# Placing the transposes of h and of a later tile of x between the products of the experts' second layer

## The chip, the cores and the metric

One core of a Trainium2 chip runs the whole program in one launch. The metric is device time in microseconds (us) of that core, as the median of several executions. The kernel before takes 1447.33 us (three runs, 1446.78 to 1450.29). One more execution was profiled; it took 1446.02 us, of which the span from the first to the last instruction is 1444.1 us. All durations below come from that execution.

The engines are named as in the profile: PE (TensorE, matrix products), PEld (the loading of PE's weights, which overlaps PE), DVE (VectorE), ACT (ScalarE), POOL (GpSimd) and SP (SyncE, which issues most DMAs).

## The reference

```python
x = attention(q, k, v)                 # 4608 tokens, 512 features
# experts: one of 8 per token
logits = x @ w_gate
e_idx  = argmax(logits)
for e in range(8):
    h  = maximum(x[mask] @ w1[e], 0)   # 512 -> 1024
    ye = h @ w2[e]                     # 1024 -> 512
    out[mask] = gate_w * eom * ye
# a dense layer pair after it
g = s * maximum(x @ w_in, 0)**2 + b    # 512 -> 2048
y = g @ w_out                          # 2048 -> 512
```

All tensors are float32. The change touches the experts only.

## The kernel before

The program has three stages on PE: attention with the router (to about 200 us of the span), the experts (200 to 680 us) and the dense pair (680 us to the end). Instructions of each engine run in the order in which the code issues them; a hand-written order decides what stands where, and no planner moves it.

The experts work on tiles of 128 tokens, sorted by expert and padded; there are 39 such tiles for these inputs. `gather(i)` (POOL, an indirect DMA) fetches tile i into one of two buffers `xg`. `tr(i)` turns it on PE: four transposes of 128x128 into the PSUM tile `pt`, which `split` (ACT, then DVE) cuts into a high and a low part `xh`, `xl` in float32r. `l1(i)` is the first layer: 24 products of 512 columns, 12 into `bank[0]` and 12 into `bank[1]`; behind the first 12 ACT makes `hs[0]` with a relu (L1032), behind the second DVE makes `hs[1]` (L1034). `trh()` turns both halves of h: eight transposes into the PSUM tiles `th0`, `th1`; `cut_h` splits these into `hh` and `hl`, which are the weights of the 24 products of the second layer, `l2` (L1058, into `py`).

The layers are skewed by one tile. One round of the loop, `slot(i)`, is on PE: the 24 products of `l1(i)`; the 24 products of `l2` for tile i-1; eight transposes of h of tile i; four transposes of x of tile i+2. From the 36th tile on the number of tiles is known only at run time: `close` and `more` write one branch (`tc.If(total > i)`) inside the other, and there the transposes of h stand first behind the branch. Behind the last of these branches `finish_h`, in the tail, turns and splits the last h, and the last second layer follows at once.

Beside PE, a round on ACT and DVE is in this order: the relus; the split of a later x; if the expert changes, four pieces of the split of new w1 (`sw1`); the copy of `py` of the round before; a step of preparing the dense weights (`side`, `db.step`, with POOL); the split of h; if the expert changes, four pieces of the split of new w2 (`sw2`); another step of `side`. So everything that `sw2` and `side` put there stands ahead of the next round's relus on ACT and DVE.

Of the kernel before, what the change touches and what calls it, by code (L numbers as in the profile page):

```python
# [9 lines left out]
F32 = mybir.dt.float32  # L10
# [17 lines left out]
DM = H * D  # L28
# [3 lines left out]
P = 128  # L32
# [476 lines left out]
NSLOT = NT + E - 1  # L509
# [293 lines left out]
def split(nc, hi, lo, raw, eng=None):  # L803
    nc.scalar.activation(out=hi, in_=raw, func=AF.Copy)  # L804
    (eng or nc.vector).tensor_tensor(out=lo, in0=raw, in1=hi.bitcast(F32), op=ALU.subtract)
# [173 lines left out]
def experts(ctx, tc, c, kp, wt, xd, ys, bank, wide, side, ahead, tail):  # L979
    nc = tc.nc  # L980
    ident = c["ident"]
    p1 = ctx.enter_context(tc.tile_pool(name="ex1", bufs=1))
    p2 = ctx.enter_context(tc.tile_pool(name="ex2", bufs=2))
    ps = ctx.enter_context(tc.tile_pool(name="exps", bufs=2, space=PSUM))
    ps1 = ctx.enter_context(tc.tile_pool(name="exps1", bufs=1, space=PSUM))


    def room(name, dt, n=2):
        return [p1.tile([P, DM], I32, name=f"{name}{i}").bitcast(dt) for i in range(n)]

    xg = room("xg", F32)
    xs = list(zip(room("xh", F32R), room("xl", F32R)))
    hs = room("hs", F32)
    hh, hl = room("hh", F32R), room("hl", F32R)

    def words(t):

        return t.bitcast(U16).rearrange("p (d w) -> p w d", w=2)

    def planes(t):  # L1000

        return t.bitcast(U16).rearrange("p (w d) -> p w d", w=2)

    def apart(dst, src, engines):
        for w, copy in enumerate(engines):
            copy(out=planes(dst)[:, w], in_=words(src)[:, w])

    def gather(i):
        nc.gpsimd.indirect_dma_start(
            out=xg[i % 2], out_offset=None, in_=xd[:, :],  # L1010
            in_offset=bass.IndirectOffsetOnAxis(ap=kp["idx"][:, i:i + 1], axis=0),
        )

    def tr(i):
        a = xg[i % 2]
        pt = ps.tile([P, DM], F32, tag="pt", name="pt")
        for k in range(4):
            nc.tensor.transpose(out=pt[:, k * P:k * P + P], in_=a[:, k * P:k * P + P], identity=ident)
        return lambda: split(nc, *xs[i % 2], pt)

    def l1(i):
        xh, xl = [x.rearrange("p (k n) -> p k n", n=P) for x in xs[i % 2]]
        wh, wl = [w.rearrange("p (k f) -> p k f", f=FE) for w in wt.a]
        for n in range(2):
            s = slice(n * 512, n * 512 + 512)
            ph = bank[n]
            for k in range(4):
                nc.tensor.matmul(ph, lhsT=xh[:, k], rhs=wh[:, k, s], start=k == 0, stop=False)  # L1028
                nc.tensor.matmul(ph, lhsT=xh[:, k], rhs=wl[:, k, s], start=False, stop=False)  # L1029
                nc.tensor.matmul(ph, lhsT=xl[:, k], rhs=wh[:, k, s], start=False, stop=k == 3)  # L1030
            if n == 0:
                nc.scalar.activation(out=hs[n], in_=ph, func=AF.Relu)  # L1032
            else:
                nc.vector.tensor_scalar(out=hs[n], in0=ph, scalar1=0.0, scalar2=None, op0=ALU.max)  # L1034

    def trh():

        th = []
        for n in range(2):
            pt = ps1.tile([P, DM], F32, tag=f"th{n}", name="th")  # L1040
            for k in range(4):
                nc.tensor.transpose(out=pt[:, k * P:k * P + P], in_=hs[n][:, k * P:k * P + P], identity=ident)  # L1042
            th.append(pt)
        return th

    def cut_h(th):
        for n in range(2):
            split(nc, hh[n], hl[n], th[n])

    def l2(py, end=False):  # L1050
        wh, wl = [w.rearrange("p (k f) -> p k f", f=DM) for w in wt.b]
        ah, al = [[h[k // 4][:, k % 4 * P:k % 4 * P + P] for k in range(8)] for h in (hh, hl)]
        steps = [[(ah[k], wh[:, k]), (ah[k], wl[:, k]), (al[k], wh[:, k])] for k in range(8)]
        if end:
            steps = [[s[0] for s in steps], [s[1] for s in steps], [s[2] for s in steps]]
        steps = [s for part in steps for s in part]
        for j, (a, w) in enumerate(steps):
            nc.tensor.matmul(py, lhsT=a, rhs=w, start=j == 0, stop=j == len(steps) - 1)  # L1058
        return py

    def room_y():
        return ps.tile([P, DM], F32, tag="py", name="py")

    def result(i, py, end=False):

        y = wide() if end else p2.tile([P, DM], F32, tag="y", name="y")
        apart(y, py, [nc.scalar.copy, nc.vector.tensor_copy])
        r = nc.values_load(kp["st"][0:1, i:i + 1], engines=[ENG.SP], min_val=0, max_val=N - 1)
        nc.sync.dma_start(out=ys[bass.ds(r, P), :], in_=y.bitcast(U16))

    def sw1(i):
        wt.switch(0, kp["chg"][0:1, i:i + 1], kp["nxt"][0:1, (i and i + 1):(i and i + 1) + 1], i == 0)

    def sw2(i):
        wt.switch(1, kp["chg"][0:1, i:i + 1], kp["nxt"][0:1, (i and i + 1):(i and i + 1) + 1], i == 0)

    def second(i):

        e = nc.values_load(kp["nxt"][0:1, 1:2], engines=[ENG.SP], min_val=0, max_val=E - 1)
        for j in range(4):  # L1080
            wt.load(i, bass.ds(e, 1), part=j)

    gather(0)
    gather(1)
    tr(0)()
    gather(2)
    sw1(0)
    tr(1)()
    gather(3)
    wt.split(1)  # L1090
    sw2(0)
    total = None


    later = []

    def first(i):
        l1(i)
        if i < 2:
            second(i)  # L1100
        if later:
            later.pop(0)()
        if i + 1 < NSLOT:
            sw1(i + 1)
        while later:
            later.pop(0)()

    def slot(i):
        first(i)
        if i >= 1:  # L1110
            py = l2(room_y())
        th = trh()
        if i + 2 < NSLOT:
            later.append(tr(i + 2))
        side(i, 0)
        gather(i + 4)
        cut_h(th)
        if i >= 1:
            sw2(i)
            later.append(lambda: result(i - 1, py))  # L1120
        side(i, 1)

    for i in range(NT - 1):
        if i == NT - 2:
            total = nc.values_load(
                kp["total"][0:1, 0:1], engines=[ENG.PE, ENG.Activation, ENG.DVE, ENG.SP, ENG.Pool],
                min_val=NT, max_val=NSLOT,
            )
        slot(i)


    py = room_y()

    def close(i):
        first(i)
        if i < NT:
            tr(i + 2)()
            gather(i + 4)
        l2(py)
        sw2(i)  # L1140

    def more(i):

        if i == NSLOT:
            return
        with tc.If(total > i):
            cut_h(trh())
            if NT < i < NSLOT - 1:
                tr(i + 1)()
                if i + 3 < NSLOT:  # L1150
                    gather(i + 3)
            result(i - 2, py)
            close(i)
            more(i + 1)

    i = NT - 1
    close(i)
    side(i, 0)
    side(i, 1)
    ahead(NT, 0)  # L1160
    more(NT)

    def finish_h():
        cut_h(trh())

    def before():
        result(NSLOT + 1, py, True)

    def second_layer():
        end = room_y()  # L1170
        l2(end, True)
        return lambda: result(NSLOT, end, True)

    tail(finish_h, before, second_layer, hs, xg, lambda: p2.tile([P, DM], F32, tag="y", name="y"))


# [55 lines left out]
class Dense:  # L1232
# [93 lines left out]
    def cut(self, j):  # L1326
        hi, lo = self.cut_steps(j)
        self.later([hi], [lo])
# [139 lines left out]
    def side(self, n, j):  # L1468


        q, p = divmod(n, NPAIR)
        if q == 0 and 1 <= p < 5 and j % 2 == 0:
            self.db.step()
        if q + 1 == NGRP:
            return
        if (n, j) == (1, 0):
            n = GT * P
            self.features(self.next, [self.next[:, 4 * n:5 * n], self.extra[:, 0:n], self.extra[:, n:2 * n]])
        plan = PLAN0 if q == 0 else PLAN
        for what, k in plan.get((p, j), []):  # L1480
            getattr(self, what)(*((q + 1, k) if what in ("load", "join") else () if k is None else (k,)))
        if p == NPAIR - 1:
            self.cut(j)
# [165 lines left out]
```

## Time and profile before

| what | value |
|---|---|
| median of three runs | 1447.33 us |
| profiled execution / its span | 1446.02 / 1444.1 us |
| PE busy, share of the span | 1412.4 us, 98% |
| DVE, ACT, POOL busy | 828.1, 709.4, 429.3 us |
| products of the second layer (L1058) | 936, median 389 ns each by their records |
| transposes of h (L1042) | 312, median 272 ns by their records |
| transposes of x (L1018) | 160, median 273 ns by their records |

The record of a PE instruction is longer than its turn, since one begins while the one before still drains. What PE can issue is read from the distance of starts, not from the records' lengths. A timeline row that merges several instructions gives the first start and the stretch to the last end.

### The profile page before, as it was taken

To read this page: it belongs to the slowest core of one execution; us is meant where nothing else is said; L and a number is where in the kernel's file an instruction comes from. 1 tells how busy PE (TensorE), PEld (TensorE's weight loads), DVE (VectorE), ACT (ScalarE), POOL (GpSimd) and SP (SyncE) were. 2 spreads that over 40 slices of the span, in tenths; PEclk is the share of its full clock that TensorE was granted. 3 is DMA by queue.
4 is the path that set the end of the run, shared out by engine and by line. 5 is a ranking of instruction groups with operands and counts; after the bars stand their busy time and mean duration, and the time that the engine had idled before them with its cause. 6 is when DMAs were issued, how large, how long until landed. Compare 5 with 4: busy or idle time off the path is not lost.

```text
span 1444.1 us, 23042 instructions
## 1 busy us (share of the span) xinstructions
PE 1412.4 (98%) x7612; PEld 1243.0 (86%) x7612; DVE 828.1 (57%) x1669; ACT 709.4 (49%) x1318; POOL 429.3 (30%) x579
## 2 busy tenths in 40 slices
PE   6999999999999999999999999999999999999998
PEld 5898978888888888887888988888888888889887
DVE  6788885487746567324666534634554463455333
ACT  3666623365534355223556555545555554555443
POOL 4998233444655558325320100000010000001001
PEclk9999999999999999999999999999999999999999
DMA  9995343277865768485665654465465446545441
GB/s 248 282 316 172 125 168 127 88 234 225 234 199 184 215 192 254 144 64 153 220 163 131 181 145 127 121 189 139 117 182 147 121 129 182 138 117 162 121 115 62
DMA packets 203040, 239.43 MB, mean 166 GB/s; under 512 B 66702, under 2 KB 114062, under 8 KB 202894
## 3 DMA queue, kind: packets, MB, share of 16 engines
q1 hardware_dynamic: 195502, 217.22, 54.2%
q0 software_dynamic: 7392, 20.49, 4.7%
q8 instruction: 63, 1.03, 0.3%
q14 instruction: 83, 0.68, 0.2%
HBM read 184.39 MB, written 43.83 MB: 158 GB/s over the span
## 4 chain that ended last, share of the span: by engine, by line
PE 44%; issue 8%; DVE 0%; ACT 0%; POOL 0%; DMA 0%; POOLq 0%; DVEq 0%; ACTq 0%
PE po L1439 8%; PE po L1438 8%; PE po L1437 7%; PE bank L1378 7%; PE bank L1379 7%; PE bank L1380 7%; PE py L1058 0%; POOL out L1449 0%; DMA ring<-ws 0%; DVE yo L1446 0%; POOLq L1645 0%; DVE y L1393 0%; ACT wb L1402 0%; DVE wb L1404 0%; ACT xg L1384 0%
## 5 line engine op out<-in xcount | busy, mean ns | idle before, releaser
L1401 ACT ACTIVATE r<-r,s_b 128x384 f32<-128x384 f32 x188 | 133.3, 709 | 275.4 <-DVE r L1394 247.8
L1449 POOL DMA_INDIRECT out<-yo,kp_pos x36 | 35.7, 991 | 662.9 <-ACT yo L1448 537.2
L1439 PE MATMUL po<-wo,wb 128*128 128x512 f32 x576 | 228.6, 397 | 0.0
L1438 PE MATMUL po<-wo,wb 128*128 128x512 f32 x576 | 227.6, 395 | 0.0
L1437 PE MATMUL po<-wo,wb 128*128 128x512 f32 x576 | 224.0, 389 | 0.0
L1058 PE MATMUL py<-wb,hh 128*128 128x512 f32 x624 | 191.2, 389 | 0.3 <-ACT hh L804 0.3
L1393 DVE TENSOR_TENSOR r<-bank,held 128x384 f32<-128x384 f32 x141 | 78.4, 556 | 183.1 <-PE bank L1380 181.1
L1378 PE MATMUL bank<-wa,ring 128*128 128x384 f32 x480 | 162.3, 338 | 1.0 <-ACT xg L1384 0.9
L1379 PE MATMUL bank<-wa,ring 128*128 128x384 f32 x480 | 162.1, 338 | 0.0
L1380 PE MATMUL bank<-wa,ring 128*128 128x384 f32 x480 | 161.0, 335 | 0.0
L1404 DVE TENSOR_TENSOR wb<-r,wb 128x384 fp32r<-128x384 f32 x188 | 105.3, 560 | 67.8 <-ACT wb L1402 67.4
L1058 PEld LDWEIGHTS py<-wb,hh 128*128 128x128 f32 x624 | 117.0, 188 | 24.7 <-ACT hh L804 0.5
L804 ACT ACTIVATE hh<-th 128x512 fp32r<-128x512 f32 x78 | 42.5, 595 | 180.1 <-PE th L1042 179.0
L1439 PEld LDWEIGHTS po<-wo,wb 128*128 128x128 f32 x576 | 107.9, 187 | 23.1
L1028 PE MATMUL bank<-wa,xh 128*128 128x512 f32 x312 | 125.5, 402 | 0.0
L931 POOL TENSOR_SCALAR dt<-dt 128x256 f32<-128x256 f32 x64 | 71.9, 1123 | 175.3 <-DVE dt L930 148.9
L1030 PE MATMUL bank<-wa,xl 128*128 128x512 f32 x312 | 122.1, 391 | 0.0
L1029 PE MATMUL bank<-wa,xh 128*128 128x512 f32 x312 | 121.6, 390 | 0.2 <-DVEq L856 0.2
L1058 PE MATMUL py<-wb,hl 128*128 128x512 f32 x312 | 120.5, 390 | 0.0
L1437 PEld LDWEIGHTS po<-wo,wb 128*128 128x128 f32 x576 | 108.2, 188 | 11.5
L1438 PEld LDWEIGHTS po<-wo,wb 128*128 128x128 f32 x576 | 107.9, 187 | 11.5
L1378 PEld LDWEIGHTS bank<-wa,ring 128*128 128x128 f32 x480 | 90.1, 188 | 16.2 <-ACT r L1390 4.6
(262 smaller groups left out, 2846.5 us busy)
## 6 DMA issues: line engine op xcount, KB each, us to landing
ring<-ws SPq DMA_DIRECT2D x336, 256.0 KB
wr<-in_moe_w SPq DMA_DIRECT2D x72, 512.0 KB
ws<-wf SPq DMA_DIRECT2D x16, 896.0 KB
ys<-y SPq DMA_DIRECT2D x37, 256.0 KB
xd<-x SPq DMA_DIRECT2D x36, 256.0 KB
q<-in_q SPq DMA_DIRECT2D x16, 512.0 KB
vr<-in_v SPq DMA_DIRECT2D x8, 1024.0 KB
dx<-in_moe_w_out SPq DMA_DIRECT2D x32, 256.0 KB
```

The costliest lines, as they stand in the source:

```text
L1028: nc.tensor.matmul(ph, lhsT=xh[:, k], rhs=wh[:, k, s], start=k == 0, stop=False)
L1029: nc.tensor.matmul(ph, lhsT=xh[:, k], rhs=wl[:, k, s], start=False, stop=False)
L1030: nc.tensor.matmul(ph, lhsT=xl[:, k], rhs=wh[:, k, s], start=False, stop=k == 3)
L1058: nc.tensor.matmul(py, lhsT=a, rhs=w, start=j == 0, stop=j == len(steps) - 1)
L1378: nc.tensor.matmul(o, lhsT=w[:, 0, k], rhs=xh[:, k], start=f, stop=False, skip_group_check=True)
L1379: nc.tensor.matmul(o, lhsT=w[:, 0, k], rhs=xl[:, k], start=False, stop=False, skip_group_check=True)
L1380: nc.tensor.matmul(o, lhsT=w[:, 1, k], rhs=xh[:, k], start=False, stop=False, skip_group_check=True)
L1401: lambda: nc.scalar.activation(out=r, in_=r, func=AF.Identity, scale=s_b[:, 0:1], bias=s_b[:, 1:2]),
L1404: [lambda: nc.vector.tensor_tensor(out=gl, in0=r, in1=gh.bitcast(F32), op=ALU.subtract)],
L1437: nc.tensor.matmul(o, lhsT=gh[:, s], rhs=wh, start=first, stop=False)
L1438: nc.tensor.matmul(o, lhsT=gh[:, s], rhs=wl, start=False, stop=False)
L1439: nc.tensor.matmul(o, lhsT=gl[:, s], rhs=wh, start=False, stop=last)
```

## The change

The four transposes of a tile become a list of steps (`turns`), which `l2` takes as `among`. `l2` issues one of them behind the 4th product, the 5th, the 7th, the 8th and so on: two of three products are followed by a transpose, until the list is used up. In a round of `slot` the list holds the eight of h and the four of x, and its last one stands behind the 20th product. In `close` it holds the eight of h alone, so they now stand ahead of the branch; those of x stay in a row (`tr_now`). In the first round, which has no second layer, they stay in a row. `th0` and `th1` are allocated once. `cut_h` stays where it was.

```diff
+    def turns(pt, a):
+        return [
+            lambda k=k: nc.tensor.transpose(out=pt[:, k * P:k * P + P], in_=a[:, k * P:k * P + P], identity=ident)
+            for k in range(4)
+        ]
     def tr(i):
-        a = xg[i % 2]
         pt = ps.tile([P, DM], F32, tag="pt", name="pt")
-        for k in range(4):
-            nc.tensor.transpose(out=pt[:, k * P:k * P + P], in_=a[:, k * P:k * P + P], identity=ident)
-        return lambda: split(nc, *xs[i % 2], pt)
+        return turns(pt, xg[i % 2]), lambda: split(nc, *xs[i % 2], pt)
...
+    th = [ps1.tile([P, DM], F32, tag=f"th{n}", name="th") for n in range(2)]
     def trh():
...
+        return [f for pt, h in zip(th, hs) for f in turns(pt, h)]
...
         for j, (a, w) in enumerate(steps):
             nc.tensor.matmul(py, lhsT=a, rhs=w, start=j == 0, stop=j == len(steps) - 1)
+            if among and j >= 2 and (j % 3 != 2 or len(among) >= len(steps) - j - 1):
+                among.pop(0)()
...
     def slot(i):
         first(i)
+        among = trh()
+        if i + 2 < NSLOT:
+            steps, cut = tr(i + 2)
+            among += steps
+            later.append(cut)
         if i >= 1:
-            py = l2(room_y())
-        th = trh()
-        if i + 2 < NSLOT:
-            later.append(tr(i + 2))
+            py = l2(room_y(), among)
+        else:
+            for f in among:
+                f()
         side(i, 0)
         gather(i + 4)
-        cut_h(th)
+        cut_h()
...
     def close(i):
         first(i)
         if i < NT:
-            tr(i + 2)()
+            tr_now(i + 2)
             gather(i + 4)
-        l2(py)
+        l2(py, trh())
         sw2(i)
     def more(i):
...
         with tc.If(total > i):
-            cut_h(trh())
+            cut_h()
...
     def finish_h():
-        cut_h(trh())
+        cut_h()
```

On PE, in a round of the loop, the end of the second layer before (`py` is the second layer's output, `th` and `pt` the turned h and x, `bank` the first layer's output):

```order
L1058 MATMUL py<-wb_2839,hh_2887 128x512
L1058 MATMUL py<-wb_2840,hh_2887 128x512
L1058 MATMUL py<-wb_2839,hl_2889 128x512
L1042 MATMUL th<-ident,hs_2884 128x128 x4
L1042 MATMUL th<-ident,hs_2885 128x128 x4
L1018 MATMUL pt<-ident,xg_2878 128x128 x4
L1028 MATMUL bank_2860<-wa_114,xh_2881 128x512
```

And of the changed kernel, on PE, the beginning of the second layer of a round (hs_2884 is `hs[0]`, made by ACT; hs_2885 is `hs[1]`, made by DVE):

```order
L1065 MATMUL py<-wb_2839,hh_2886 128x512
L1017 MATMUL th<-ident,hs_2884 128x128
L1065 MATMUL py<-wb_2840,hh_2886 128x512
L1017 MATMUL th<-ident,hs_2884 128x128
L1065 MATMUL py<-wb_2839,hl_2888 128x512
L1065 MATMUL py<-wb_2839,hh_2886 128x512
L1017 MATMUL th<-ident,hs_2885 128x128
L1065 MATMUL py<-wb_2840,hh_2886 128x512
```

The transposes moved from behind the 24th product to places from behind the 4th to behind the 20th: the first that reads `hs[0]` stands 20 products earlier, the first that reads `hs[1]` 14 products earlier.

On PE in the tail, behind the last branch, before:

```order
L1146 UNCONDITIONAL_BRANCH x7
L1042 MATMUL th<-ident,hs_2884 128x128 x4
L1042 MATMUL th<-ident,hs_2885 128x128 x4
L1058 MATMUL py<-wb_2839,hh_2886 128x512 x4
L1058 MATMUL py<-wb_2839,hh_2887 128x512 x4
```

And on PE at the same place in the changed kernel:

```order
L1160 UNCONDITIONAL_BRANCH x7
L1065 MATMUL py<-wb_2839,hh_2886 128x512 x4
L1065 MATMUL py<-wb_2839,hh_2887 128x512 x4
```

The eight transposes of the last h are no longer between the branch and the last second layer.

## Rows read from the trace of the kernel before

**Rows 1.** Page, part 1: busy us, share of the span, instructions.
```profile
PE 1412.4 (98%) x7612; PEld 1243.0 (86%) x7612; DVE 828.1 (57%) x1669; ACT 709.4 (49%) x1318; POOL 429.3 (30%) x579
```

**Rows 2.** Windows, 33 rounds: stretch, length, PE PEld DVE ACT POOL busy, PEclk, DMA.
```profile
220.98:625.13 404.15, 404.15 (x1984) 339.13 (x1982) 248.54 (x415) 182.06 (x309) 208.87 (x232) 1.00 0.63 184
```

**Rows 3.** Timeline of PE, one round: start us, length us, engine, line, tiles, count.
```profile
300.04 0.61 PE L1058 MATMUL py<-wb,hh 128*128 128x512 f32 x2
...
305.25 0.40 PE L1058 MATMUL py<-wb,hl 128*128 128x512 f32 x1
305.48 1.04 PE L1042 MATMUL th<-ident,hs 128*128 128x128 f32 x8
306.36 0.60 PE L1018 MATMUL pt<-ident,xg 128*128 128x128 f32 x4
306.71 0.47 PE L1028 MATMUL bank<-wa,xh 128*128 128x512 f32 x1
307.03 0.39 PE L1029 MATMUL bank<-wa,xh 128*128 128x512 f32 x1
...
309.11 0.39 PE L1029 MATMUL bank<-wa,xh 128*128 128x512 f32 x1
...
318.96 0.48 PE L1028 MATMUL bank<-wa,xh 128*128 128x512 f32 x1
```

**Rows 4.** Timeline of PEld: loads of four transposes within the row.
```profile
306.25 0.47 PEld L1018 LDWEIGHTS pt<-ident,xg 128*128 128x128 f32 x4
```

**Rows 5.** Timeline of the first round, where transposes waited for the second relu.
```profile
207.15 0.69 DVE L1034 TENSOR_SCALAR hs<-bank 128x512 f32<-128x512 f32 x1
...
207.89 0.42 PEld L1042 LDWEIGHTS th<-ident,hs 128*128 128x128 f32 x4 [0.97 <-DVEq L856]
207.89 0.66 PE L1042 MATMUL th<-ident,hs 128*128 128x128 f32 x4 [0.73 <-DVEq L856]
```

**Rows 6.** Timeline of PE: where the second layer begins in four rounds.
```profile
324.53 0.61 PE L1058 MATMUL py<-wb,hh 128*128 128x512 f32 x2
...
471.49 0.39 PE L1058 MATMUL py<-wb,hh 128*128 128x512 f32 x1
...
544.97 0.39 PE L1058 MATMUL py<-wb,hh 128*128 128x512 f32 x1
...
557.22 0.39 PE L1058 MATMUL py<-wb,hh 128*128 128x512 f32 x1
```

**Rows 7.** Timeline of ACT and DVE: the relus of these rounds (three of ACT).
```profile
325.76 0.58 ACT L1032 ACTIVATE hs<-bank 128x512 f32<-128x512 f32 x1
...
327.80 0.68 DVE L1034 TENSOR_SCALAR hs<-bank 128x512 f32<-128x512 f32 x1
...
473.95 0.68 DVE L1034 TENSOR_SCALAR hs<-bank 128x512 f32<-128x512 f32 x1
...
546.99 0.57 ACT L1032 ACTIVATE hs<-bank 128x512 f32<-128x512 f32 x1
...
549.07 0.68 DVE L1034 TENSOR_SCALAR hs<-bank 128x512 f32<-128x512 f32 x1
...
560.39 0.58 ACT L1032 ACTIVATE hs<-bank 128x512 f32<-128x512 f32 x1
...
561.53 0.68 DVE L1034 TENSOR_SCALAR hs<-bank 128x512 f32<-128x512 f32 x1
```

**Rows 8.** Timeline: what ran ahead of the late relus on ACT and POOL.
```profile
306.12 1.09 ACT L804 ACTIVATE hh<-th 128x512 fp32r<-128x512 f32 x2 [2.56 <-PE th L1042]
...
546.12 0.96 ACT L804 ACTIVATE wf<-wf 128x896 fp32r<-128x896 f32 x1 [2.09 <-POOL wf L976]
...
553.85 5.65 POOL L976 TENSOR_TENSOR wf<-wf 128x128 f32<-128x128 f32 x4
```

**Rows 9.** Timeline of PE behind the last branch: the last transposes and second layer.
```profile
673.69 1.06 PE L1042 MATMUL th<-ident,hs 128*128 128x128 f32 x8 [0.62 <-PEq L1146]
675.06 1.20 PE L1058 MATMUL py<-wb,hh 128*128 128x512 f32 x4 [0.30 <-ACT hh L804]
```

More of the change, by code (lines that the diff above doesn't have):

```diff
@@ L1012, in gather, with tr_now @@
         )
+    def turns(pt, a):
[3 more added lines that the diff above has]
+        ]
     def tr(i):
-        a = xg[i % 2]
         pt = ps.tile([P, DM], F32, tag="pt", name="pt")
-        for k in range(4):
-            nc.tensor.transpose(out=pt[:, k * P:k * P + P], in_=a[:, k * P:k * P + P], identity=ident)
-        return lambda: split(nc, *xs[i % 2], pt)
+        return turns(pt, xg[i % 2]), lambda: split(nc, *xs[i % 2], pt)
+    def tr_now(i):
+        steps, cut = tr(i)
+        for f in steps:
+            f()
+        cut()
     def l1(i):
@@ L1034, in l1, with cut_h, l2 @@
                 nc.vector.tensor_scalar(out=hs[n], in0=ph, scalar1=0.0, scalar2=None, op0=ALU.max)
+    th = [ps1.tile([P, DM], F32, tag=f"th{n}", name="th") for n in range(2)]
     def trh():
[L1038 to L1046, printed above, removed]
+        return [f for pt, h in zip(th, hs) for f in turns(pt, h)]
+    def cut_h():
         for n in range(2):
             split(nc, hh[n], hl[n], th[n])
-    def l2(py, end=False):
+    def l2(py, among=(), end=False):
+        among = list(among)
         wh, wl = [w.rearrange("p (k f) -> p k f", f=DM) for w in wt.b]
@@ L1084, in experts @@
     gather(1)
-    tr(0)()
+    tr_now(0)
     gather(2)
     sw1(0)
-    tr(1)()
+    tr_now(1)
     gather(3)
@@ L1109, in slot @@
         first(i)
+        among = trh()
[3 more added lines that the diff above has]
+            later.append(cut)
         if i >= 1:
-            py = l2(room_y())
-        th = trh()
-        if i + 2 < NSLOT:
-            later.append(tr(i + 2))
+            py = l2(room_y(), among)
+        else:
+            for f in among:
+                f()
         side(i, 0)
         gather(i + 4)
-        cut_h(th)
+        cut_h()
         if i >= 1:
@@ L1146, in more @@
         with tc.If(total > i):
-            cut_h(trh())
+            cut_h()
             if NT < i < NSLOT - 1:
-                tr(i + 1)()
+                tr_now(i + 1)
                 if i + 3 < NSLOT:
@@ L1170, in second_layer @@
         end = room_y()
-        l2(end, True)
+        l2(end, end=True)
         return lambda: result(NSLOT, end, True)
```

## The prediction

> **What bounds the kernel now.** I read the page's busy shares first: PE is busy 98% of the span [rows 1]. That alone doesn't say that every stretch hangs on PE, so I took the windows of the 33 rounds of the expert loop: PE is busy 404.15 of 404.15 us at a granted clock of 1.00 (the 2.4 GHz level), while DVE has 61%, ACT 45%, POOL 52% [rows 2]. In these rounds PE never waits. Whatever the change adds to PE's issue, or makes PE wait, therefore lengthens the run one for one, as the dense stage behind it is not waiting for anything that arrives by clock time. What waits in these rounds is ACT and DVE, for PE.
>
> Then I read one round by its starts [rows 3]. Products of 512 columns follow each other at 5.21 us / 23 = 0.2265 us (300.04 to 305.25). Eight transposes take 305.48 to 306.36, 0.110 us each; the finer value from the loads below is 0.109. A round is 12.25 us (306.71 to 318.96); 48 products and 12 transposes at these paces are 10.87 + 1.31 = 12.18. The missing 0.07 lies around the row of transposes: 0.23 instead of 0.2265 into it, and behind it nine products from 307.03 to 309.11 at 0.231 each, 0.04 over; two hundredths of that are rounding of starts.
>
> **Part 1: PE's pace.** 34 rounds of the loop move 12 transposes each, four `close` rounds move 8 each: 440 in all. None is removed. Is one cheaper when it stands alone between products? Its load already hides behind the product in front of it (the row begins 0.23 after the last product), and in the row the transposes follow at 0.109, not held by their loads: where PE had waited for the second relu, four loads took 0.42 us from first begin to last end [rows 5], against 0.47 within a row [rows 4], so the first two were 0.06 apart, while the four transposes took 0.66 [rows 5] against 0.60 in a row [rows 3]. The load needs about 0.06, the transpose itself 0.109. The product behind it needs its own load meanwhile; the product behind the last transpose of a row began really at about 306.80 (its successor at 307.03 less one pace), which is 0.11 behind that transpose. So a lone transpose still costs 0.11, and I see no gain.
>
> There is a small loss. Products near transposes run at 0.231 instead of 0.2265, and the row's entrance costs 0.005. With transposes behind two of three products, the 18 products from the 4th to the 21st are all near one: 18 x 0.0045 = 0.08, and 12 entrances and exits of about 0.005 in place of one pair, partly the same time. I take 0.10 per round (0.07 with eight): 34 x 0.10 + 4 x 0.07 = **+3.7 us**. Bounds: 0, if a lone transpose leaves the pace alone; and 0.25 per round, 8.5 us, if each leaves twice what the row shows. A whole 0.07 for each lone one (26 us) is not possible, since most of it lies on nine following products and here one or two follow. I take the value next to the measured 0.231.
>
> The products of the first layer behind it keep a disturbed stretch as before, since the last transpose stands only four products ahead of them.
>
> **Part 2: waits for the relus.** Before, the first transpose stood 24 products behind the first layer. Now the first of `hs[0]` stands behind the 4th product of the second layer and the first of `hs[1]` behind the 10th product and four transposes. With S the start of the second layer, PE gets there at S + 4 x 0.2265 = S + 0.91 and at S + 10 x 0.2265 + 4 x 0.109 = S + 2.70. From a relu's end to the transpose pass 0.05 (207.84 to 207.89), and its load of 0.06 is then in the open [rows 5]: 0.11. In most rounds both relus are long done: ACT's and DVE's wait only for the bank. But where w2 of a new expert is being split, or `side`'s pieces pile up, they come late. Four rounds matter; S from [rows 6], the relus' ends from [rows 7]:
>
> - S = 324.53: hs[0] ends 326.34, wanted 325.44: 0.90 + 0.11 = 1.01. hs[1] ends 328.48, wanted 327.23 + 1.01 = 328.24: 0.35 more. Together 1.4.
> - S = 471.49: hs[1] ends 474.63, wanted 474.19: 0.55.
> - S = 544.97: hs[0] ends 547.56, wanted 545.88: 1.79. hs[1] ends 549.75, wanted 549.46 after that wait: 0.40. Together 2.2.
> - S = 557.22: hs[0] ends 560.97, wanted 558.13: 2.95; hs[1] at 562.21 is then in time.
>
> Two corrections. First, `hh[1]` can no longer begin behind the transposes; it must wait until the last product has read the old one. Before, the pair of splits ended at 307.21 [rows 8], 0.41 behind the round's real start. Now the last product drains 0.16 into the round, plus 0.03 and one split of about 0.6: 0.8. ACT's chain behind it (the split of w2, then the relu) is 0.39 later where nothing else holds it, as at 471.49: 0.55 + 0.39 = 0.9. In the other three it is held otherwise: at 544.97 ACT waited 2.09 us for POOL's sums of the dense weights just ahead of the relu [rows 8]. Second, PE reaches the round of 557.22 some 2.2 us later because of the wait before it, while the POOL sums that end at 559.50 [rows 8] and hold ACT there don't wait for PE. That leaves 0.75 for hs[0]; DVE's own chain, which starts from `hh` and so from PE, moves along, and makes hs[1] late instead. Between 0.75 and 2.95 I take 2.0, nearer to the upper row, because DVE's splits dominate there.
>
> Sum: 1.4 + 0.9 + 2.2 + 2.0 = **+6.5 us** (bounds 4.9 and 8.5). Behind the waiting transpose on PE's queue stand the rest of the second layer and the whole next round; nothing passes it.
>
> **Part 3: what becomes earlier.** In the tail the eight transposes are gone from behind the last branch. Before, the last began at 673.69 + 1.06 - 0.27 = 674.48; the second layer could have followed at 674.59 and did at 675.06, for want of `hh` [rows 9]. ACT will have split it while PE still finishes the layer before and crosses the branch: **-0.5 us**. The 0.62 us at the branch stays. Elsewhere the branches show no gap that the transposes filled. `hh[0]` and the x tile's split are ready sooner, but nothing waits for them: the next reader is a first layer away. The transposes of x come about 1.8 us earlier and the gather for them was issued two rounds, 24.5 us, before: nothing. POOL's next gather can start sooner; nothing waits for it either. No DMA is added or moved on SP's queue.
>
> **Sum.** 3.7 + 6.5 - 0.5 = 9.7 on the profiled execution's 1446.02: 1455.7. The median of the runs is 1.31 above that execution, so I forecast 1457.0.
>
> **Rivals.**
> - *The transposes were held by their loads, and alone they hide* (faster). Each would give back the part of 0.109 that its load needs beyond its own pass. By the two stretches of loads (0.47 and 0.42) that part is 0.05: 440 x 0.05 = 22 us, 1425. For it: the same work, spread over products under which loads hide. Against it: the loads that came 0.06 apart, and the following product's load, which takes the transpose's place as the holder. It decides from a lone transpose costing under 0.09. The Trainium skill ("TensorE: Matmul & The Clock Gate", LDWEIGHTS) gives columns / 1.2, 107 ns for 128 columns, and under "Back-to-back issue gap" 56 ns for a pass of 128 columns; by these a row would be held by its loads at about the pace seen, and lone ones would save up to 51 ns each, an estimated 22 us. The trace disagrees on which of the two is the long one.
> - *The relus arrive in time*, since the waits of PE shift or DVE's earlier `hl[0]` pulls its chain forward. Only the pace is lost: 1447.33 + 3.7 - 0.5 = 1450.5. For it: DVE's first split of h can move up. Against: ACT's late relus hang on POOL and on w2.
> - *Nothing moves*: the slow products are not due to the transposes, and the waits are absorbed: 1447.
> - *Waits spread*: each of seven expert changes pays what the worst round shows, 7 x 2.95 = 20.7, plus 3.2: 1471. Against: most changes leave the relus early enough.
>
> **How the numbers follow.** The forecast (waits and pace) 0.66; in-time relus 0.14; nothing 0.08; faster by hidden loads 0.04; spread waits 0.08. What a measurement of this kernel can tell from no change is 0.3%, 4.3 us, that is up to 1451.7. The forecast's own bounds are 4.9 + 0 - 0.5 = 4.4 and 8.5 + 8.5 - 0.5 = 16.5, 1451.7 to 1463.8; the in-time case ends at 1450.5. Range 1449 to 1464, which leaves out the faster case, no change and most of the spread. Slower: the forecast less 0.01 and the spread, 0.73. Within: the in-time case and nothing, with the forecast's lowest end, 0.22. Faster: 0.05.
>
> **What would show it.** In the profile after: a lone transpose between two products adds 0.11 to 0.12 to the distance of their starts (0.06 would prove the first rival); a quiet round takes 12.30 to 12.40 instead of 12.25; PE has idle time before transposes of h put down to the two relus, of 1 to 3 us in rounds that lie near 325, 545 and 557; the last second layer starts with hardly a wait behind the branch. Wrong would be: quiet rounds shorter than 12.2, or no idle time at these rounds.

## The result, and the profile after

The changed kernel takes 1455.8 us (median of six runs, 1454.78 to 1458.01), the kernel before 1447.62 us beside it (six runs, 1446.59 to 1450.29). The ratio is 1.0055, 95% interval 1.0042 to 1.0068: 8.2 us slower. Forecast was 1457.0, in a range of 1449 to 1464.

The profiled execution has a span of 1453.9 us, 9.8 over that of before. Of these, 1.0 lie ahead of the first round of the experts (its first product starts at 201.52, before at 200.51), in code that the change doesn't touch (in the traces of the first four variants below, that start lies between 199.05 and 201.45); 8.8 lie behind that, nearly all in the rounds. From the first round's products on, the two traces can be compared stretch by stretch.

First the stretch of [rows 2] in the changed kernel: the same 33 rounds, with the same columns.

```profile
222.18:634.89 412.71, 409.16 (x1981) 326.83 (x1980) 248.95 (x415) 184.76 (x308) 204.66 (x233) 1.00 0.62 180
```

It is 412.71 us in place of 404.15: 8.6 of the 8.8. PE is no longer busy throughout, 3.55 us of idle time have come in, and the granted clock is still 1.00. So there are two losses: idle time, and 5.0 us in which PE is busy with the same instructions for longer.

The view of waits of the changed kernel, PE from the first round on, says whom the idle time is put down to (us in total, times, longest):

```profile
PE th L1017 <- ACT hs L1042: 2.3, 3, 1.5
PE th L1017 <- DVE hs L1044: 1.1, 3, 0.5
PE py L1065 <- ACT hh L804: 1.0, 1, 1.0
PE th L1017 <- DVEq L856: 0.7, 1, 0.7
```

The first two are the relus, in the places that the prediction named; the third is the tail; the last is the first round, which waits for its second relu before as well ([rows 5]). To size a wait, idle time is not enough: the product ahead of it drains about 0.16 us into the idle stretch, and the load of the transpose stands in the open behind it. The rounds' lengths show both. A quiet round takes 12.353 us (median of 33 rounds in the trace, by the start of its first product); the five rounds that are longer take 0.89 (near 326), 0.15 (near 364), 0.73 (near 476), 2.01 (near 550) and 1.35 us more (near 565), 5.1 in all. So of the 8.6 us in [rows 2]'s stretch 5.1 are waits and 3.4 are a slower pace.

The longest wait, on the timeline of PE and of ACT, the round that answers to the third of [rows 6] and [rows 7]:

```profile
550.52 0.62 PE L1065 MATMUL py<-wb,hh 128*128 128x512 f32 x2
...
551.20 0.39 PE L1065 MATMUL py<-wb,hh 128*128 128x512 f32 x1
553.06 0.33 PE L1017 MATMUL th<-ident,hs 128*128 128x128 f32 x1 [1.47 <-ACT hs L1042]
...
555.25 0.33 PE L1017 MATMUL th<-ident,hs 128*128 128x128 f32 x1
```
```profile
551.57 0.95 ACT L804 ACTIVATE wf<-wf 128x896 fp32r<-128x896 f32 x1 [1.73 <-POOL wf L976]
552.42 0.58 ACT L1042 ACTIVATE hs<-bank 128x512 f32<-128x512 f32 x1
```

The second layer begins at 550.52 and reaches the first transpose at 551.43; the relu ends at 553.00, and the transpose starts at 553.06. As before, ACT's relu stood behind a split that waited for POOL's sums. The other 20 products of the layer, and all that follows, stood behind the transpose on PE's queue.

Now the other half, a quiet round on PE's timeline (it answers to [rows 3]):

```profile
408.46 0.40 PE L1038 MATMUL bank<-wa,xh 128*128 128x512 f32 x1
...
414.60 0.40 PE L1065 MATMUL py<-wb,hh 128*128 128x512 f32 x1
414.83 0.28 PE L1017 MATMUL th<-ident,hs 128*128 128x128 f32 x1
414.86 0.48 PE L1065 MATMUL py<-wb,hh 128*128 128x512 f32 x1
415.18 0.27 PE L1017 MATMUL th<-ident,hs 128*128 128x128 f32 x1
415.20 0.48 PE L1065 MATMUL py<-wb,hl 128*128 128x512 f32 x1
415.52 0.39 PE L1065 MATMUL py<-wb,hh 128*128 128x512 f32 x1
...
420.82 0.40 PE L1038 MATMUL bank<-wa,xh 128*128 128x512 f32 x1
```

Three products and two lone transposes take 414.60 to 415.52, 0.92 us; three products at 0.2265 and two transposes at 0.109 would be 0.90. A product "starts" 0.03 behind the transpose, but that is only its record: it is 0.48 long in place of 0.39. When it really began is seen on the timeline of the loads:

```profile
414.60 0.14 PEld L1017 LDWEIGHTS th<-ident,hs 128*128 128x128 f32 x1
414.83 0.19 PEld L1065 LDWEIGHTS py<-wb,hh 128*128 128x128 f32 x1
414.97 0.14 PEld L1017 LDWEIGHTS th<-ident,hs 128*128 128x128 f32 x1
415.18 0.19 PEld L1065 LDWEIGHTS py<-wb,hl 128*128 128x128 f32 x1
415.29 0.19 PEld L1065 LDWEIGHTS py<-wb,hh 128*128 128x128 f32 x1
```

In these rows a load begins when the instruction ahead of it takes its turn, not earlier. The transpose's load hides behind the product (414.60, used at 414.83). The product's load begins with the transpose (415.18), and the next load, which marks the product's own beginning, comes 0.11 later (415.29). Where the next load is a transpose's it comes 0.14 later (414.83 to 414.97), so the mark is good to about 0.03. So the transpose costs its 0.11 alone as well as in a row.

### The profile page after: what moved, and what is told of

Its sections match the earlier page's. It is cut to its first block, busy times and chain, and to the rows that moved or that the text cites. A ratio compares the mean times of both kernels' runs of the same rounds, so it can differ in the third digit from the quotient of the medians.

```text
span 1453.9 us, 23119 instructions
## 1 busy us (share of the span) xinstructions
PE 1414.1 (97%) x7612; PEld 1225.6 (84%) x7612; DVE 829.7 (57%) x1669; ACT 712.7 (49%) x1318; POOL 424.6 (29%) x579
## 4 chain that ended last, share of the span: by engine, by line
PE 43%; issue 8%; ACT 1%; POOL 0%; SPq 0%; DMA 0%; DVE 0%; POOLq 0%; ACTq 0%; DVEq 0%
PE po L1453 8%; PE po L1452 8%; PE po L1451 7%; PE bank L1392 7%; PE bank L1393 7%; PE bank L1394 7%; POOL out L1463 0%; DMA ring<-ws 0%; SPq L1379 0%; ACT wb L1416 0%; ACT y L1415 0%; ACT r L1415 0%; POOLq L1659 0%; ACT yo L1462 0%; ACT xg L1398 0%
## 5 line engine op out<-in xcount | busy, mean ns | idle before, releaser
L1065 PE MATMUL py<-wb,hh 128*128 128x512 f32 x624 | 220.1, 424 | 1.0 <-ACT hh L804 1.0
L804 ACT ACTIVATE hh<-th 128x512 fp32r<-128x512 f32 x78 | 46.6, 599 | 191.5 <-PE py L1065 176.6
L1065 PE MATMUL py<-wb,hl 128*128 128x512 f32 x312 | 139.7, 451 | 0.0
L1039 PE MATMUL bank<-wa,xh 128*128 128x512 f32 x312 | 121.6, 390 | 0.3 <-DVEq L856 0.3
L1038 PE MATMUL bank<-wa,xh 128*128 128x512 f32 x312 | 121.9, 391 | 0.0
L805 DVE TENSOR_TENSOR hl<-th,hh 128x512 fp32r<-128x512 f32 x78 | 52.8, 686 | 94.8 <-ACT hh L804 53.9
```

## The experiments

Each of the first four ran beside the kernel before, on one chip (1447.32 us, median of 35 runs). "Quiet round" is the median length of the 33 rounds in the run's trace, and "waits" the sum of what longer rounds take above it. In the kernel before, the rounds alternate between 12.252 and 12.241: median 12.252, mean 12.247. Each variant has one profiled execution, so its waits are those of one execution.

### Same places, x first

This is the run x_first.

```diff
-            among += steps
+            among = steps + among
```

> The changed kernel with the same 12 places, but the four transposes of x take the first four places and the eight of h the last eight. The pattern of lone transposes is the same, only what they wait for is later. Theory (waits for the relus and a slower pace, each its own term): a quiet round stays at 12.35 us as in the changed kernel, and the waits shrink, since hs[0] is now wanted at S + 2.75 and hs[1] at S + 4.55: nothing in the rounds near 326 and 476, about 0.2 in the one near 550, 1.0 to 1.4 in the one behind it; 1.2 to 1.6 in all in place of 5.1. Median about 1452.5 (1447.6 + 3.7 + 1.4). Rival 1 (all of the loss is waits, the pace only looks slower): about 1449. Rival 2 (all of the loss is pace, the idle time is given back later): 1455.8 as the changed kernel.

Measured: 1450.55 us, ratio 1.0021 (1.0010 to 1.0032). Quiet round 12.353, as in the changed kernel; waits 0.19 and 0.75 in the rounds that answer to the last two of [rows 6], 0.94 in all, a little under what was expected. The view of waits of this run has one relu left:

```profile
PE py L1065 <- ACT hh L804: 0.8, 1, 0.8
PE th L1017 <- ACT hs L1042: 0.5, 1, 0.5
```

The pattern of lone transposes costs the same and the waits are nearly gone, so the two terms are separate. Neither is given back elsewhere: from the start of the stretch of [rows 2] to the end of the trace this run takes 4.4 us more than the kernel before, and its 33 rounds alone 4.5. So both rivals fall, the first by the trace alone: its 1449 lies inside the interval of the median, and the 1452.5 of the theory just outside. The median moved by 5.2 from the changed kernel's 1455.8; by waits it should have moved by 4.2, and the two were not timed side by side. One of the waits that are gone is not to the credit of the places: near 326 the relu of `hs[0]` ends only 0.10 behind the second layer's start in this run, in time for the old places too (see Waits below).

### All in a row behind the 10th product

This is the run row_early.

```diff
-            if among and j >= 2 and (j % 3 != 2 or len(among) >= len(steps) - j - 1):
+            while among and j == 9:
```

> All 12 transposes (eight in the branches) in one row behind the 10th product of the second layer. Theory: the pace is that of the kernel before (quiet round 12.25 us), but the waits are there: hs[0] wanted at S + 2.27, hs[1] at S + 2.70, which gives about 1.0 to 1.3 in the round near 326, 0.8 near 476, 2.1 near 550 and 1.4 to 2.0 in the one behind it: 5.3 to 6.3 us in all, median 1452.9 to 1453.9. Rival 1 (all pace): 1447.6. Rival 2 (a row in the middle of the second layer slows the products on both sides, also without waits): a quiet round above 12.30.

Measured: 1451.02 us, ratio 1.0023 (1.0009 to 1.0036). Quiet round 12.247; waits 0.80, 0.20, 0.81, 2.16 and 0.80 in the same five rounds, 4.8 in all, under the 5.3 to 6.3 that were expected, because the last of them came out at 0.80 in place of 1.4 to 2.0; the median is 2 to 3 us under. PE's timeline in the worst round:

```profile
550.35 0.66 PE L1017 MATMUL th<-ident,hs 128*128 128x128 f32 x4 [0.21 <-ACT hs L1042]
552.53 0.66 PE L1017 MATMUL th<-ident,hs 128*128 128x128 f32 x4 [1.53 <-DVE hs L1044]
```

The waits are there without a single lone transpose, now mostly for DVE's relu. And a row in the middle of the second layer is no dearer than one behind it: the pace depends on the row being whole, not on its place.

### Only ahead of the branches

This is the run row_last.

```diff
-            if among and j >= 2 and (j % 3 != 2 or len(among) >= len(steps) - j - 1):
+            while among and j == len(steps) - 1:
```

> The changed kernel's code with all transposes in one row behind the last product, so that only one part of the change is left: in the branches the transposes of h stand ahead of the branch, not behind it. Theory: a quiet round 12.25 us, no waits for the relus, the time of the kernel before within 1 us (1446.6 to 1448.6). Rival (the move ahead of the branches carries a part of the loss or gives something back): 1 us or more beside it, visible in the rounds from the 36th on and in the tail.

Measured: 1447.23 us, ratio 0.9997 (0.9985 to 1.0009). Quiet round 12.252, no waits; 36th to 38th round 12.295, 12.225 and 12.253, to the nanosecond those of before. Placing the transposes of h ahead of the branches carries nothing of the loss.

### Pairs

```diff
-            if among and j >= 2 and (j % 3 != 2 or len(among) >= len(steps) - j - 1):
+            for _ in range(2 if j % 3 == 1 and j >= 3 else 0):
```

> The transposes stand in pairs, behind the 5th, 8th, 11th, 14th, 17th and 20th product (six pairs, four in the branches), otherwise the changed kernel. Theory as in the prediction (each product near a transpose runs at 0.231 in place of 0.2265, whatever stands between): all products from the 5th to the 23rd are still near one, a quiet round 12.33 to 12.35. Rival (the loss is paid per change between transposes and products): six changes in place of twelve, a quiet round 12.28 to 12.30. The waits are a little smaller than in the changed kernel, since hs[0] is wanted at S + 1.13 and hs[1] at S + 2.95: 4 to 5 us. Median 1454 to 1455.5 by the theory, 1452.5 to 1453.5 by the rival.

Measured: 1451.8 us, ratio 1.0035 (1.0022 to 1.0047). Quiet round 12.307; waits 0.53, 1.86 and 0.69, 3.1 in all, under the 4 to 5 that were expected: near 326 there is none, since the relu of `hs[0]` ends 0.10 behind the second layer's start in this run too. The timeline of a quiet round, two starts of the first layer and one pair:

```profile
404.37 0.39 PE L1038 MATMUL bank<-wa,xh 128*128 128x512 f32 x1
...
410.94 0.38 PE L1017 MATMUL th<-ident,hs 128*128 128x128 f32 x2
411.08 0.48 PE L1065 MATMUL py<-wb,hl 128*128 128x512 f32 x1
411.39 0.63 PE L1065 MATMUL py<-wb,hh 128*128 128x512 f32 x2
411.86 0.38 PE L1017 MATMUL th<-ident,hs 128*128 128x128 f32 x2
...
416.67 0.39 PE L1038 MATMUL bank<-wa,xh 128*128 128x512 f32 x1
```

Over 12.247 of one row, that is 0.060 with six stretches of transposes and 0.106 with twelve: 0.012 and 0.010 for each stretch beyond the first. The round lies outside both ranges, as the median lies under both, nearer the rival's 12.28 to 12.30 than the prediction's 12.33 to 12.35. So the loss goes mostly with the number of changes between transposes and products. Products near transposes are slow in this run as well: the two from 411.39 to the pair at 411.86 take 0.235 each. The part on the pace below sets the two against each other.

### Only x, alone, and what holds a transpose

Three runs (x_lone, x_row_16 and x_lone_16), each timed once (1446.67, 1442.65 and 1451.57 us beside 1446.64); the rounds' lengths carry the verdict. In the first, the four transposes of x stand alone, and h stays in a row behind the last product.

```diff
+            if among and j >= 15 and j % 3 != 2:
+                among.pop(0)()
...
+            py = l2(room_y(), steps)
+        for f in trh():
+            f()
```

> Only the four transposes of x stand alone among the products (behind the 16th, 17th, 19th and 20th); those of h are in one row behind the last product, in the branches too. Theory (0.009 us per change between a transpose and products, as the pairs showed): four changes more than the kernel before, a quiet round 12.28 to 12.30 us, no wait for a relu. Rival (the prediction's wording: products near transposes run slow): seven products near them, 12.28 as well at the low end, but then the two runs below must lie apart from it by whole passes.

Quiet round 12.287 (12.273 and 12.287 alternate), no waits: four stretches more, 0.008 to 0.009 each. This is at the low end of what the theory expects and is the rival's 12.28 as well, so this run alone does not tell them apart.

In the second and third, the transposes of x were replaced by 2-byte ones of a constant tile, in the row and alone.

```diff
+            lambda k=k: nc.tensor.transpose(out=pb[:, k * P:k * P + P], in_=c["ones"], identity=id16)
```

> Order of the kernel before, but from the third tile on the four transposes of x are replaced by four of a constant 2-byte tile (left out: the turning of x; its layers then compute on constants). It measures what holds transposes in a row. Theory (a row is held by each transpose's own pass, 0.109 for 4 bytes, about 0.055 for 2): three of the four shorten, the fourth is still held by the 0.11 load of the product behind it: a quiet round 12.08 to 12.12 us. Rival (loads hold the row, and a load takes as long as before): 12.25.

> As the run x_lone, with the same 2-byte transposes in place of those of x, each alone among the products (left out: the turning of x). Theory (behind a lone transpose the next product waits for its own weights, whose load of 0.11 begins only when the transpose begins, so that the pass no longer matters): a lone one still costs 0.11 to 0.12, and a quiet round stays at 12.26 to 12.31, about 0.2 above the row of the same transposes. Rival (a lone transpose costs its own pass): 12.08 to 12.12.

The row, on PE's timeline, with the round's two starts:

```profile
402.97 0.48 PE L1048 MATMUL bank<-wa,xh 128*128 128x512 f32 x1
...
414.00 1.04 PE L1017 MATMUL th<-ident,hs 128*128 128x128 f32 x8
414.87 0.39 PE L1030 MATMUL pt<-tri,ones 128*128 128x128 bf16 x4
415.07 0.48 PE L1048 MATMUL bank<-wa,xh 128*128 128x512 f32 x1
```

Quiet round 12.093, 0.159 under the 12.252 of the kernel before: three transposes shorter by 0.053, and the fourth not, as expected. The four and the lead of the next product's record take 0.20 in place of 0.35. And alone:

```profile
408.40 0.47 PE L1048 MATMUL bank<-wa,xh 128*128 128x512 f32 x1
...
417.60 0.23 PE L1030 MATMUL pt<-tri,ones 128*128 128x128 bf16 x1
417.64 0.48 PE L1075 MATMUL py<-wb,hh 128*128 128x512 f32 x1
417.96 0.23 PE L1030 MATMUL pt<-tri,ones 128*128 128x128 bf16 x1
...
420.75 0.48 PE L1048 MATMUL bank<-wa,xh 128*128 128x512 f32 x1
```

From one transpose to the next across a product it is 0.36, with 4-byte transposes 0.35 (414.83 to 415.18). The quiet rounds alternate between 12.349 and 12.324, above the expected 12.26 to 12.31 and 0.23 to 0.26 above the row of the same transposes. (Both of these runs also have a few longer rounds, 2.4 and 1.7 us in all, whose cause stays open.) So a transpose that is half as long saves nothing when it stands alone.

That the load of the following product's weights holds its place is seen at the end of the row, on the timeline of the loads in x_row_16:

```profile
414.76 0.32 PEld L1030 LDWEIGHTS <-ones 128*128 128x128 bf16 x4
415.04 0.19 PEld L1048 LDWEIGHTS bank<-wa,xh 128*128 128x128 f32 x1
415.15 0.19 PEld L1049 LDWEIGHTS bank<-wa,xh 128*128 128x128 f32 x1
```

The product's load begins with the last 2-byte transpose (415.04), and the product itself 0.11 later (415.15), as behind a 4-byte one, though the transpose passes in 0.056. How long such a load takes by itself the kernel before shows in its tail, where PE had waited and nothing stood ahead: two loads of products begin 0.108 apart (675.057 and 675.165), two loads of 4-byte transposes 0.057 (673.660 and 673.717). The lone run by itself could not tell, because there the transpose's own load is not hidden:

```profile
417.96 0.10 PEld L1030 LDWEIGHTS <-ones 128*128 128x128 bf16 x1 [0.15 <-issue]
417.96 0.20 PEld L1075 LDWEIGHTS py<-wb,hl 128*128 128x128 f32 x1
```

It begins only with its transpose (417.96), where that of a 4-byte one began with the product ahead. That may be why a lone 2-byte one costs another 0.014 over a 4-byte one; no run tests it.

The Trainium skill ("TensorE: Matmul & The Clock Gate", "Back-to-back issue gap" and "LDWEIGHTS") has 56 ns for a pass of 128 columns and, as columns / 1.2, 107 ns for the load of 128 columns. The first agrees with the 2-byte transposes (0.056 in the row), the second with the products' loads here (0.108); the loads of the transposes are shorter (0.057), and neither figure is the 0.109 of the kernel's own 4-byte transposes in their row, which is their pass.

### Splitting h ahead of the branches

This is the run x_first_cut: x_first with one more edit, for the tail.

```diff
         l2(py, trh())
+        cut_h()
         sw2(i)
...
     def finish_h():
-        cut_h()
+        pass
```

> The run x_first with the split of h moved ahead of the branches and of the tail. Theory (in the changed kernel the split of h behind a branch waits for all of PE's work ahead of the branch, so the last second layer waits for it): hh[0] is cut while PE still works, and the last second layer follows the last product of the layer before after about 1.0 us in place of 1.36: 0.3 to 0.5 us less in the tail, the median within noise of x_first (1449.8 to 1451), still above the kernel before. Rival (the 1.36 is PE's own way across the branches): unchanged 1.36.

Measured: 1451.04 us, ratio 1.0036 (1.0024 to 1.0047), beside 1446.64 of before. The tail on PE's timeline:

```profile
676.81 0.40 PE L1065 MATMUL py<-wb,hl 128*128 128x512 f32 x1
678.23 2.09 PE L1065 MATMUL py<-wb,hh 128*128 128x512 f32 x8 [1.03 <-ACTq L1161]
681.53 2.11 PE L1065 MATMUL py<-wb,hh 128*128 128x512 f32 x8 [1.21 <-DVEq L1161]
```

The split is done early (ACT's starts at 677.06 in this run's timeline and takes 0.60), but the last second layer starts 1.43 us behind the last product all the same, and PE stops once more for 1.21. What it waits for is named by the queue, as far as the profile can infer it: ACT's and DVE's own crossing of the branches (L1161). Expected was 1.0 in place of 1.36; the rival said unchanged, for PE's way alone. In the trace of x_first itself, without this edit, it is 1.23 and there is no second stop. So the edit gains nothing: in this trace the tail is 1.6 us longer by it.

No variant beats the kernel before. Of those that keep its work, row_last is level with it; x_lone's one timing is too, but its 33 rounds take 1.1 us more.

## Why the prediction was right, and where it was off

**Pace.** Forecast +3.7: 0.10 per round of 12, 0.07 per `close`. Measured: 12.353 against 12.247 (the mean of the rounds before, one of which is in [rows 3]), 0.106, and about 0.05 for the `close` rounds. The 33 rounds lose 3.4 by it (8.57 less 5.13 of waits), with the second round and the `close` rounds it is 3.7. That a lone transpose costs its 0.11 was right and is shown by the loads and by the end of the 2-byte row. What the term was made of was wrong, and that its size came out is luck. It added 0.08 for 18 products that run slow near transposes, and little for the changes.

By the starts on PE's records it is the other way round. Take what crosses a stretch of transposes, from the last product ahead of it to the second behind it or to the next stretch, less 0.2267 for each product and 0.109 for each transpose. In a quiet round that is 0.143 us over in the twelve stretches of the changed kernel, 0.073 in the six of the pairs, 0.052 in the five of x_lone and 0.017 in the one of before, so about 0.01 for each short stretch. All other steps from product to product are slow behind a stretch, as the prediction read, but hardly more so than before: 0.026 over in all in the changed kernel, 0.049 with pairs, 0.043 in x_lone, 0.044 before. The prediction took off nothing for those of before, and held that the first layer keeps its disturbed stretch; it begins with two or three slow products now, in place of nine. A crossing includes the product directly behind the stretch, so there the slow product and the change are not told apart, and why a change costs this stays open.

**Waits.** Forecast +6.5, measured 5.1, in the rounds that were named and in one more that was left out (0.15): 0.89, 0.73, 2.01 and 1.35 came for 1.4, 0.9, 2.2 and 2.0. The upper bound of 8.5 does not follow from its rows, whose most is 1.4 + 0.9 + 2.2 + 2.95 = 7.5. The step that was oversized most is the last: 2.0 us for the round of 557.22, where 1.35 came. I let DVE's chain move along with PE, which it did, but I kept the durations of before. On the timeline of POOL in the changed kernel:

```profile
559.28 1.84 POOL L976 TENSOR_TENSOR wf<-wf 128x128 f32<-128x128 f32 x4
```

The four sums took 1.84 us, against 5.65 in [rows 8]. Before, DVE's splits of w2 ran beside them; now these start at 561.07, since `hh` came later. So POOL released ACT early: the relu ended at 566.51, 1.64 behind the second layer's start, near the 1.55 that the lower bound's 0.75 rests on (560.97 less 557.22, less 2.2), and DVE's at 568.89. The other traces bear this out. In row_early and pairs, which also wait about 2 us in the round ahead, the sums take 1.84 and this relu ends 0.6 to 0.7 behind the start; in row_last, x_first and x_lone, which wait 0.2 us there or not at all, the sums take 5.6 to 5.7 and it ends 3.4 to 3.7 behind.

In the first round of [rows 6] the relu ended 1.23 behind S, before 1.81. What held ACT there is a DMA that brings the new w2. On the timeline of ACT, first of the kernel before, then of row_last:

```profile
322.91 1.06 ACT L804 ACTIVATE wb<-wr 128x1024 fp32r<-128x1024 f32 x1 [1.55 <-DVE wb L805]
324.17 1.06 ACT L804 ACTIVATE wb<-wr 128x1024 fp32r<-128x1024 f32 x1 [0.20 <-SPq L856]
```
```profile
319.78 3.90 ACT L804 ACTIVATE wb<-wr 128x1024 fp32r<-128x1024 f32 x4
324.22 0.58 ACT L1042 ACTIVATE hs<-bank 128x512 f32<-128x512 f32 x1
```

The last two pieces landed at 322.76 and 324.06, 1.77 and 0.47 ahead of S, and ACT began to split each 0.1 to 0.15 later; in the changed kernel they landed at 324.33 and 325.03, 2.05 and 1.35 ahead of S (326.38 there). (The profile puts the first of these waits down to DVE; in row_last ACT goes on without waiting for DVE.) In row_last, whose rounds are as long as those of before, ACT splits all four without a stop, and the relu ends 0.15 ahead of S (324.96) in place of 1.81 behind it; in x_first and pairs it ends 0.10 behind. So this term of 1.4 was read from what one execution happened to show, and the 0.89 is as little fixed by the places of the transposes. Why the DMA lands later in some executions stays open.

**Tail.** Forecast -0.5, measured nothing: from the last product ahead of the branches to the last second layer it was 2.375 before and is 1.359 now, and eight lone transposes take 0.995 in the layer ahead. (In x_first, with the same code there, it is 1.23, and in row_last, with eight transposes in a row ahead, 2.10: 0.1 to 0.3 us can come back, not 0.5.) The step that failed is "ACT will have split it while PE still finishes". In the changed kernel:

```profile
683.58 0.40 PE L1065 MATMUL py<-wb,hl 128*128 128x512 f32 x1
684.94 3.94 PE L1065 MATMUL py<-wb,hh 128*128 128x512 f32 x16 [0.96 <-ACT hh L804]
```
```profile
684.29 1.09 ACT L804 ACTIVATE hh<-th 128x512 fp32r<-128x512 f32 x2 [8.78 <-PEq L1160]
```

ACT's split, behind the branch in the code, waits for PE's queue to have crossed it (PEq L1160), and PE then waits for the split ([rows 9] had the transposes in that time).

The terms add up: 3.7 + 5.1 - 0 = 8.8 by the trace, 8.2 by the medians. The rival of hidden loads (1425) fell by the loads' distances and the end of the 2-byte row; in-time relus and no change fell by the five long rounds; of seven expert changes only five rounds paid, so the waits did not spread.

## What to carry to other kernels

Before interleaving small PE instructions with large ones, look for what would hold each when alone: here a transpose's load hid behind the product ahead of it, but the next product's load then started only with the transpose, so nothing is won where that load is as long. An instruction moved earlier on an in-order queue needs its input earlier in every round, the worst one too: read the inputs' arrival per round, not the mean idle time, which here was zero, and in more than one execution, since an input that hangs on a DMA can be late in one and early in the next. Where a wait shifts other engines' work, durations that come from contention shift as well.

## What the runs showed of the hardware that was not expected

- Four additions of 128x128 on POOL took 1.83 to 1.84 us where DVE was at no split of w2 (in three traces: after, row_early, pairs), and 4.66 to 5.70 us beside those splits (in all eight traces with the work of the kernel before). With it the splits are slower too: 2.36 us for two of 128x1024, and 5.73 to 5.82 for four beside the additions.
- A transpose of 4 bytes passes 128 columns in 0.109 us, one of 2 bytes in 0.056; each stretch of transposes between float32r products costs about 0.01 us beside them.
- With nothing ahead of them, the weights of two float32r products load 0.108 us apart and those of two 4-byte transposes 0.057. The load of a lone 2-byte transpose did not begin with the product ahead of it, that of a 4-byte one did.
- Behind nested branches, PE waited for other engines' crossing, by the releasers that the profile infers: 1.0 us for ACT's and 1.2 for DVE's in one run, where the data had been ready.
